# q and k of the first batch loaded as 2 KB runs and transposed head by head against the identity, with 14 unread matmuls ahead

## The chip, the cores and the metric

The kernel runs on one core of one Trainium2 chip. The metric is the device time of one execution in microseconds (us). Before the change three runs took 983.35, 987.0 and 985.17 us, median 985.17 us.

## The reference

An attention with two branches feeds a two-layer perceptron. Batch B = 8, heads H = 8, sequence S = 576, head dimension D = 64, inner width 2048, all in float32. The "down" branch averages q, k and v over groups of 4 tokens and attends over the 144 averages; the local branch lets each token attend to the 7 tokens around it.

```python
q_d = q.reshape(B, H, Sd, factor, D).mean(axis=3)     # k_d, v_d alike; factor 4, Sd 144
out_up = np.repeat(sm_attn(q_d, k_d, v_d), factor, axis=2)
mask = np.abs(pos[:, None] - pos[None, :]) < factor
scores = np.where(mask, scale * np.matmul(q, k.transpose(0, 1, 3, 2)), -1000000000.0)
x = (out_up + softmax(scores) @ v).transpose(0, 2, 1, 3).reshape(B * S, H * D)
h = x @ w_in
g = np.maximum(h, 0.0) + alpha * np.minimum(h, 0.0)
return g @ w_out
```

The weights arrive as 64-bit numbers and are decoded to float32 on the core.

## The kernel before, in words

The 4608 token rows are cut into 18 chunks of 256. For each chunk the perceptron runs in 8 steps, so there are 144 steps in all. `hidden` (L775) of a step does 24 matmuls of 128x256 (L784) for w_in, in three terms: high part by high part, high by low, low by high. `slopes` (L788) evacuates the result on ACT (ScalarE): two rows `t` (L799) and two rows `sh` (L801, in the early steps). `larger` (L807) adds them, in the early steps on POOL (GpSimd, L76), `split` (L813) makes the high part `gh` on ACT (L816) and the low part `gl` on POOL (L73), and `product` (L833) does 12 matmuls of 128x512 (L845) for w_out. The inputs `xh` and `xl` of the perceptron are the high and low part of the attention's output.

**Decoding the weights** (`make`, L175). Each of 16 blocks (8 of w_in, 8 of w_out, 1 MB raw each) goes through ACT (`magnitude`, L197), four DVE (VectorE) rows into the tile `temp` (L201, L202, L206, L207), ACT (`upper`, L212 or L216) and DVE (`lower`, L220 or twice L224). Raw data comes through three buffers, so the DMA of a block waits on the queue of SP (SyncE) until the block three earlier has been read. The first five blocks of each matrix are decoded in the first stage.

**The first batch** (`first_batch`, L385) is done differently from the other seven, on PE (TensorE), head pair by head pair, and it fills chunks 0 and 1. `load_pair` (L411) loads q, k and v of two heads. Each of q and k comes in two DMAs, one per head, into a tile laid out as (72 partitions, q or k, 8 tokens, 2 heads, 64): a partition holds 8 tokens, and each run that a descriptor carries is one token of one head, 64 floats or 256 bytes. The v of both heads comes in one DMA with runs of 8 tokens, 2048 bytes. `load_windows` (L421) loads v again in windows of 70 keys, in runs of 256 bytes. `pair` (L441) then does, for each head pair:

- q and k transposed on PE (L447): for each of 8 tokens one transpose of 72x128 (both heads at once), four to a PSUM tile, the tiles `f0T` (q) and `f1T` (k); ACT copies them to `qb` (L451) and `kT` (L455);
- window scores on PE: the mask by an identity matrix `unit` (L463), then q by k (L467);
- the sums over 4 tokens, folded in place on DVE in two rows each: q and k in L475 and L477, v in L493 and L495; then `fsum` (L482), down scores `fsd` (L491) and their softmax (`down_probs`, L339);
- the window softmax on DVE (L503 to L510) and ACT (L506), its transposes `fpt` (L515), the products `fdv` (L523) and `fpv` (L531), and on DVE the sum of both branches `fxs` (L534); ACT makes `xh` of it (L540) and DVE `xl` (L541).

**The order of the work.** `ORDER` (L40) lists the loads of the first batch on SP's queue: `i0` is a block of w_in, `o0` one of w_out, `a` a `load_pair`, `b` a `load_windows`. SP issues DMAs in that order and each waits for its buffer. All compute of the first stage and every event with a due time under `LISTED` = 14 (L50) is handed to a scheduler that works out the order of each engine's instructions; from step 14 on the order is that of the event list, written down by hand. Each engine works through its own order strictly, and a row that waits holds up all that stand behind it.

The down branch of the second batch (`down`, L237) starts inside the first stage: loads `ld` on SP (L247), folds on POOL (L76).

Of the kernel before, what the change touches and what calls it, by code (L numbers as in the profile page):

```python
# [9 lines left out]
F32 = mybir.dt.float32  # L10
# [3 lines left out]
ALU = mybir.AluOpType  # L14
# [9 lines left out]
HEAD = S * D  # L24
SEG = 18
NF = DF // 128
T = 256
# [21 lines left out]
FAR = {3: 2, 4: 2, 5: 2, 6: 2}  # L49
LISTED = 14  # L50
JOINS = (0.04, 0.06)


@with_exitstack
def tile_attention_moe(ctx: ExitStack, tc: tile.TileContext, q, k, v, w_in, w_out, alpha, out):
    nc = tc.nc

    const = ctx.enter_context(tc.tile_pool(name="const", bufs=1))
    one = ctx.enter_context(tc.tile_pool(name="one", bufs=1))
# [3 lines left out]
    ps_h = ctx.enter_context(tc.tile_pool(name="ps_h", bufs=2, space=PS))  # L63
    ps_a = ctx.enter_context(tc.tile_pool(name="ps_a", bufs=1, space=PS))

    def bank(kind, name):
        return ps_a.tile([128, 512], F32, tag=f"p{kind}", name=name, bufs=2 if kind == "d" else 1)
# [18 lines left out]
    ident = const.tile([128, 128], F32, name="ident")  # L86
# [298 lines left out]
    def first_batch(st):  # L385
# [13 lines left out]
        unit = st.tile([128, 128], F32R, name="unit")  # L399
# [9 lines left out]
        qk, vt, vw = {}, {}, {}  # L409

        def load_pair(hp):  # L411
            qk[hp] = one.tile([72, 2, 8, 2, 64], F32, tag=f"spare{(4, 5, 0, 1)[hp]}", name=f"fqk{hp}")
            for i, src in enumerate((q, k)):
                for e in range(2):
                    nc.sync.dma_start(qk[hp][:, i, :, e, :],
                                      bass.AP(src.tensor, (2 * hp + e) * HEAD, [[512, 72], [64, 8], [1, 64]]))
            vt[hp] = st.tile([72, 2, 8, 64], F32, tag="vt", name=f"fv{hp}", bufs=3)
            nc.sync.dma_start(vt[hp].rearrange("p h t d -> p h (t d)"),
                              bass.AP(v.tensor, 2 * hp * HEAD, [[512, 72], [HEAD, 2], [1, 512]]))
# [14 lines left out]
        def pair_bank(kind, name):  # L434
            if kind == "o":
                return ps_o.tile([128, 512], F32, tag="po", name=name)
            if kind == "h":
                return ps_h.tile([128, 512], F32, tag="ph", name=name)
            return bank(kind, name)

        def pair(hp):  # L441
            halves = [slice(64 * e, 64 * e + 64) for e in range(2)]
            for x in range(2):
                for t0, nt in ((0, 4), (4, 4)):
                    ps = ps_h.tile([128, 512], F32, tag="ph", name=f"f{x}T{hp}{t0}")[:, 0:72 * nt]
                    for i in range(nt):
                        nc.tensor.transpose(ps[:, 72 * i:72 * i + 72],  # L447
                                            qk[hp][:, x, t0 + i].rearrange("p h d -> p (h d)"), ident[:72, :72])
                    if x == 0:
                        for e, r in enumerate(halves):  # L450
                            nc.scalar.copy(  # L451
                                qb[r, :, e, :].rearrange("p w (a t) -> p w a t", t=8)[:, :, :, t0:t0 + nt],
                                ps[r].rearrange("p (t w a) -> p w a t", t=nt, w=NWIN))
                    else:
                        nc.scalar.copy(  # L455
                            kT[:, 3:S + 3].rearrange("p (a t) -> p a t", t=8)[:, :, t0:t0 + nt],
                            ps.rearrange("p (t a) -> p a t", t=nt))
            for part in ("sd", "ds")[EM[hp] == "b"]:
                if part == "s":
                    banks = []  # L460
                    for w0, nw in ((0, 7), (7, 2)):
                        ps = bank("q" if w0 == 0 else "l", f"fs{hp}{w0}")
                        nc.tensor.matmul(ps[:, 0:KEYS * nw], unit,  # L463
                                         wmask[:, w0:w0 + nw].rearrange("p w j -> p (w j)"), start=True, stop=False)
                        for i in range(nw):
                            w = w0 + i
                            nc.tensor.matmul(ps[:, KEYS * i:KEYS * i + KEYS], qb[:, w].rearrange("p e i -> p (e i)"),  # L467
                                             kT[:, WIN * w:WIN * w + KEYS], start=False, stop=(i == nw - 1))
                        banks.append((w0, w0 + nw, ps[:, 0:KEYS * nw].rearrange("p (w j) -> p w j", j=KEYS)))
                else:  # L470
                    sums = []
                    for i, x in enumerate("qk"):
                        lv = qk[hp][:, i].rearrange("p (g f) h d -> p g (f h d)", g=2)
                        s4 = lv[:, :, 0:256]
                        nc.vector.tensor_tensor(s4, lv[:, :, 0:256], lv[:, :, 256:512], op=ALU.add)  # L475
                        s2 = st.tile([72, 2, 128], F32, tag=f"fs2{x}", name=f"fs2{x}{hp}")
                        nc.vector.tensor_tensor(s2, s4[:, :, 0:128], s4[:, :, 128:256], op=ALU.add)  # L477
                        sums.append(s2)
                    ps = ps_h.tile([128, 512], F32, tag="ph", name=f"fsum{hp}")
                    for x in range(2):  # L480
                        for g in range(2):
                            nc.tensor.transpose(ps[:, (2 * x + g) * 72:(2 * x + g) * 72 + 72], sums[x][:, g],  # L482
                                                ident[:72, :72])
                    for e, r in enumerate(halves):
                        nc.scalar.mul(qd[r, :, 48 * e:48 * e + 48].rearrange("p b (i g) -> p b i g", g=2),
                                      ps[r, 0:144].rearrange("p (g b i) -> p b i g", g=2, b=3), DSCALE)
                    kd = st.tile([128, 144], F32, tag="fkh", name=f"fkd{hp}")
                    nc.scalar.copy(kd, ps[:, 144:288])
                    sd = bank("d", f"fsd{hp}")[:96, 0:432].rearrange("p (b c) -> p b c", b=3)
                    for bl in range(3):  # L490
                        nc.tensor.matmul(sd[:, bl, :], qd[:, bl, :], kd, start=True, stop=True)  # L491
            lv = vt[hp].rearrange("p h (g f) d -> p (h g) (f d)", g=2)
# [8 lines left out]
            p = st.tile([128, NWIN, KEYS], F32, tag="p", name=f"fp{hp}", bufs=2)  # L501
            for a_, b_, s in banks:
                nc.vector.tensor_reduce(out=mx[:, a_:b_], in_=s, axis=AX.X, op=ALU.max)  # L503
                nc.vector.tensor_tensor(p[:, a_:b_], s, mx[:, a_:b_].unsqueeze(2).to_broadcast([128, b_ - a_, KEYS]),
                                        op=ALU.subtract)
# [6 lines left out]
            for w0, nw in ((0, 4), (4, 4), (8, 1)):  # L512
                ps = pair_bank(FPT[hp][w0 // 4], f"fpt{hp}{w0}")
# [6 lines left out]
            for g in range(2):  # L520
                for e, r in enumerate(halves):
                    pr = th[g].rearrange("p (b e a) -> p b e a", b=3, e=2)[:, :, e]
                    nc.tensor.matmul(po[r, 0:144].rearrange("p (b a) -> p b a", b=3), vd[:, e, g], pr,  # L523
                                     start=(g == 0), stop=(g == 1))
            odf = st.tile([128, SD], F32, tag="odf", name=f"fod{hp}")
            nc.scalar.copy(odf, po[:, 0:144])
            for w0, nw in ((0, 4), (4, 4), (8, 1)):
                ps = pair_bank(FPV[hp][w0 // 4], f"fpv{hp}{w0}")
# [13 lines left out]
            yield  # L542

        return load_pair, load_windows, pair


# [340 lines left out]
    with tc.tile_pool(name="start", bufs=1) as start:  # L887
        load_pair, load_windows, pair = first_batch(start)
        todo = [(w, fp) for fp in range(NP) for w in range(2)]
        for step in ORDER.split():  # L890
            kind, i = step[0], int(step[1])
# [39 lines left out]
    t = T0_DEC  # L931
# [7 lines left out]
    for p in range(4 * (B - 1)):  # L939
        b, hp = 1 + p // 4, p % 4  # L940
# [12 lines left out]
    def flip_at(u, i, t, flip):  # L953
        when_flipped[u, i] = t
        at(t, flip, i)

    put = None
    for u in range(3, 3 * B + 1):
# [7 lines left out]
        elif put and u == 4:  # L966
            for i in range(2):
                flip_at(u - 1, i, begin[u] + 0.02 + 0.01 * i, flip)
                put(i, begin[u] + JOINS[i])
        elif put:  # L970
# [66 lines left out]
```

## Time and profile before

| | |
|---|---|
| median of three runs | 985.17 us |
| the profiled execution: its own time | 982.8 us |
| its span, first to last instruction | 981.0 us |
| PE matmul busy | 942.9 us (96%) |
| PE weight loads busy | 842.0 us (86%) |
| DVE busy | 819.5 us (84%) |
| ACT busy | 555.3 us (57%) |
| POOL busy | 527.6 us (54%) |
| mean granted TensorE clock | 0.976 |
| DMA packets | 63197, of these 23556 under 512 bytes |

All stretches and rows below are times from the span's start. A row of the timeline gives its start and its length in us, the engine, the line, the operation with its tiles, the count, and in brackets how long the engine was idle before it and what ended that. A row of the table by stretches gives, after the stretch and its length, the busy time of PE, PEld (weight loads), DVE, ACT and POOL with the number of instructions, the granted clock, the mean busy share of the 16 DMA engines and GB/s. One float32 matmul is two records on PE; a transpose, and a matmul on float32r operands (all of L463, L784 and L845), is one. PE's records overlap, so the pace of a group is its length over its count, and not the mean length of one.

### The profile page before, as it was taken

The numbers are of one execution on the slowest core, as the hardware profiler recorded it, in microseconds if no ns is written. First come the engines' busy times: TensorE is split into PE (matmuls) and PEld (weight loads), VectorE is DVE, ScalarE is ACT, GpSimd is POOL, SyncE is SP. The second block draws the span as 40 slices with busy tenths as digits, with TensorE's granted clock in tenths as the row PEclk, the third lists the DMA queues.
The fourth block names the chain that finished last, engine by engine and source line by source line (L and its number), as shares of the span: only waits on it lengthen the run. The fifth ranks groups of instructions, "written<-read, shape, count | busy, mean of one in ns | idle before, by whom it ended". The sixth has DMA issues, their size and how long they took to land.

```text
span 981.0 us, 17943 instructions
## 1 busy us (share of the span) xinstructions
PE 942.9 (96%) x6402; PEld 842.0 (86%) x6402; DVE 819.5 (84%) x1318; ACT 555.3 (57%) x1483; POOL 527.6 (54%) x642
## 2 busy tenths in 40 slices
PE   5878999999999999999999999999999999999998
PEld 4757887987888888989988899898899989999997
DVE  7999978888879999998889899899898889997111
ACT  4767776544645655556554655565556664544442
POOL 2055877787887546555537365555466633323221
PEclk9956999999999999999999999999999999999999
DMA  8946723132333322422322423332333321310000
GB/s 200 232 146 208 254 90 107 61 114 85 111 101 116 114 76 88 139 80 83 119 78 86 127 86 93 108 98 68 105 112 103 110 63 46 97 34 22 1 22 22
DMA packets 63197, 98.28 MB, mean 100 GB/s; under 512 B 23556, under 2 KB 28932, under 8 KB 63108
## 3 DMA queue, kind: packets, MB, share of 16 engines
q1 hardware_dynamic: 62916, 96.88, 32.8%
q8 instruction: 50, 0.82, 0.3%
q10 hardware_dynamic: 192, 0.26, 0.1%
q14 instruction: 39, 0.32, 0.1%
HBM read 87.67 MB, written 9.44 MB: 99 GB/s over the span
## 4 chain that ended last, share of the span: by engine, by line
PE 59%; DVE 11%; POOL 4%; ACT 3%; issue 2%; DMA 1%; SPq 0%; DVEq 0%; POOLq 0%
PE o L845 28%; PE h L784 27%; DVE lb L673 3%; DVE pv L670 2%; DVE qk L614 1%; PE s L278 1%; PE pv L312 1%; DVE t L811 1%; DVE ls L618 1%; PE xp L682 1%; POOL t L76 1%; PE pT L302 1%; DVE xf L698 1%; ACT t L799 1%; POOL gl L73 1%
## 5 line engine op out<-in xcount | busy, mean ns | idle before, releaser
L73 POOL TENSOR_TENSOR gl<-t,gh 128x512 fp32r<-128x512 f32 x144 | 186.3, 1294 | 323.4 <-ACT gh L816 303.3
L799 ACT ACTIVATE t<-h,slope 128x256 f32<-128x256 f32 x288 | 136.3, 473 | 128.8 <-PE h L784 105.7
L845 PE MATMUL o<-woh,gh 128*128 128x512 f32 x576 | 192.8, 405 | 2.5 <-ACT gh L816 1.1
L784 PE MATMUL h<-xh,wih 128*128 128x256 f32 x1152 | 188.0, 285 | 2.6 <-ACT sh L801 1.9
L845 PE MATMUL o<-wol,gh 128*128 128x512 f32 x576 | 185.7, 393 | 0.0
L845 PE MATMUL o<-woh,gl 128*128 128x512 f32 x576 | 185.4, 393 | 0.0
L784 PE MATMUL h<-xh,wil 128*128 128x256 f32 x1152 | 180.7, 279 | 0.0
L784 PE MATMUL h<-xl,wih 128*128 128x256 f32 x1152 | 180.5, 279 | 0.0
L784 PEld LDWEIGHTS h<-xh,wih 128*128 128x128 f32 x1152 | 162.8, 190 | 13.0 <-ACT sh L801 2.6
L816 ACT CAST gh<-t 128x512 fp32r<-128x512 f32 x144 | 89.5, 622 | 140.3 <-DVE t L811 81.6
L76 POOL TENSOR_TENSOR ld<-ld 72x256 f32<-72x256 f32 x168 | 131.9, 787 | 67.4 <-DMA ld<-in_q 64.8
L784 PEld LDWEIGHTS h<-xh,wil 128*128 128x128 f32 x1152 | 155.3, 190 | 0.3
L784 PEld LDWEIGHTS h<-xl,wih 128*128 128x128 f32 x1152 | 154.6, 190 | 0.1
L811 DVE TENSOR_TENSOR t<-h,t 128x512 f32<-128x512 f32 x114 | 78.3, 687 | 88.2 <-ACT h L803 87.8
L618 DVE TENSOR_REDUCE ls<-qk 128x12 f32<-128x768 f32 (+1 forms) x126 | 136.2, 1083 | 3.1
L845 PEld LDWEIGHTS o<-woh,gl 128*128 128x128 f32 x576 | 108.0, 188 | 24.0
L845 PEld LDWEIGHTS o<-wol,gh 128*128 128x128 f32 x576 | 108.0, 188 | 23.1 <-DVE temp L207 0.2
L673 DVE TENSOR_TENSOR lb<-lb,pv 128x384 f32<-128x384 f32 x202 | 114.0, 564 | 5.9
L845 PEld LDWEIGHTS o<-woh,gh 128*128 128x128 f32 x576 | 99.1, 188 | 18.9 <-issue 2.6
L803 ACT ACTIVATE h<-h,sign 128x256 f32<-128x256 f32 x228 | 100.2, 439 | 0.0
L670 DVE TENSOR_TENSOR pv<-v,lb 128x1152 f32<-128x1152 f32 x84 | 93.6, 1115 | 2.7
L614 DVE TENSOR_TENSOR qk<-k,qp 128x768 f32<-128x768 f32 (+1 forms) x78 | 84.0, 1078 | 4.6 <-ACT qp L607 4.6
(151 smaller groups left out, 1185.7 us busy)
## 6 DMA issues: line engine op xcount, KB each, us to landing
k<-in_k SPq DMA_DIRECT2D x41, 384.0 KB
v<-in_v SPq DMA_DIRECT2D x41, 384.0 KB
out<-sg SPq DMA_DIRECT2D x140, 64.0 KB
raw<-in_moe_w_in SPq DMA_DIRECT2D x16, 512.0 KB
raw<-in_moe_w_out SPq DMA_DIRECT2D x16, 512.0 KB
ld<-in_q SPq DMA_DIRECT2D x56, 144.0 KB
ld<-in_k SPq DMA_DIRECT2D x56, 144.0 KB
ld<-in_v SPq DMA_DIRECT2D x56, 144.0 KB
```

What stands on the lines that cost most here:

```text
L73: nc.gpsimd.tensor_tensor(o, a, b, op=ALU.subtract)
L76: nc.gpsimd.tensor_tensor(o, a, b, op=ALU.add)
L614: nc.vector.tensor_tensor(st["pr"][:, :nd], window(tiles[u, "k"], half, d0, nd), st["qp", half].unsqueeze(1).to_broadcast([128, nd, 2, 192 ...
L618: nc.vector.tensor_reduce(out=st["s"][:, half, d0:d0 + nd, :].rearrange("p a b -> p (a b)"), in_=st["pr"][:, :nd].rearrange("p a h (t d) - ...
L670: nc.vector.tensor_tensor(st["pr"][:, :nd], window4(tiles[u, "v"], half, d0, nd), prob(half, d0, nd), op=ALU.mult)
L673: nc.vector.tensor_tensor(st["acc"], st["acc"], st["pr"][:, i], op=ALU.add)
L784: nc.tensor.matmul(ph[:, j], w[:, m, 128 * o:128 * o + 128], x[:, m, :], start=(i == 0), stop=(i == 11))
L799: nc.scalar.activation(t[:, j], hs[st][:, j], AF.Copy, scale=slope[:, f:f + 1])
L803: nc.scalar.activation(other[:, j], hs[st][:, j], AF.Copy, scale=sign[:, f:f + 1])
L811: nc.vector.tensor_tensor(gs[st], hs.pop(st), gs[st], op=ALU.max)
L816: nc.scalar.copy(gh, t)
L845: nc.tensor.matmul(outs[c][m], g[:, j, 128 * m:128 * m + 128], wo[w][n][:, o, :], start=(f == 0 and i == 0), stop=(f == NF - 1 and i == 2))
```

## The change

The two DMAs for q of a head pair become one, with runs of 2048 bytes, and so do those for k. The tile is laid out head by head: (72, q or k, 2 heads, 8 tokens, 64), as that of v already is. In place of one transpose for both heads stand two float32 matmuls, one per head, of 64 columns against the identity, each into its own half of PSUM's partitions. The DVE folds of q and k go over the same 512 and 256 elements for each partition in the new layout. Ahead of the very first q tile, 14 matmuls of 128x512 multiply `unit` by itself into the same PSUM tile, which is then written over.

```diff
+WARM = 14
...
         def load_pair(hp):
-            qk[hp] = one.tile([72, 2, 8, 2, 64], F32, tag=f"spare{(4, 5, 0, 1)[hp]}", name=f"fqk{hp}")
+            qk[hp] = one.tile([72, 2, 2, 8, 64], F32, tag=f"spare{(4, 5, 0, 1)[hp]}", name=f"fqk{hp}")
             for i, src in enumerate((q, k)):
-                for e in range(2):
-                    nc.sync.dma_start(qk[hp][:, i, :, e, :],
-                                      bass.AP(src.tensor, (2 * hp + e) * HEAD, [[512, 72], [64, 8], [1, 64]]))
+                nc.sync.dma_start(qk[hp][:, i].rearrange("p h t d -> p h (t d)"),
+                                  bass.AP(src.tensor, 2 * hp * HEAD, [[512, 72], [HEAD, 2], [1, 512]]))
...
-                    ps = ps_h.tile([128, 512], F32, tag="ph", name=f"f{x}T{hp}{t0}")[:, 0:72 * nt]
+                    ps = ps_h.tile([128, 512], F32, tag="ph", name=f"f{x}T{hp}{t0}")
+                    if (hp, x, t0) == (0, 0, 0):
+                        for _ in range(WARM):
+                            nc.tensor.matmul(ps.rearrange("p (a n) -> p a n", a=4), unit,
+                                             unit.unsqueeze(1).to_broadcast([128, 4, 128]), start=True, stop=True)
+                    ps = ps[:, 0:72 * nt]
                     for i in range(nt):
-                        nc.tensor.transpose(ps[:, 72 * i:72 * i + 72],
-                                            qk[hp][:, x, t0 + i].rearrange("p h d -> p (h d)"), ident[:72, :72])
+                        for e, r in enumerate(halves):
+                            nc.tensor.matmul(ps[r, 72 * i:72 * i + 72], qk[hp][:, x, e, t0 + i], ident[:72, :72], start=True, stop=True)
...
-                        lv = qk[hp][:, i].rearrange("p (g f) h d -> p g (f h d)", g=2)
-                        s4 = lv[:, :, 0:256]
-                        nc.vector.tensor_tensor(s4, lv[:, :, 0:256], lv[:, :, 256:512], op=ALU.add)
+                        lv = qk[hp][:, i].rearrange("p h (g f) d -> p (h g) (f d)", g=2)
+                        s4 = lv[:, :, 0:128]
+                        nc.vector.tensor_tensor(s4, lv[:, :, 0:128], lv[:, :, 128:256], op=ALU.add)
                         s2 = st.tile([72, 2, 128], F32, tag=f"fs2{x}", name=f"fs2{x}{hp}")
-                        nc.vector.tensor_tensor(s2, s4[:, :, 0:128], s4[:, :, 128:256], op=ALU.add)
+                        s4 = s4.rearrange("p (h g) c -> p h g c", h=2)
+                        nc.vector.tensor_tensor(s2.rearrange("p g (h d) -> p h g d", h=2), s4[:, :, :, 0:64], s4[:, :, :, 64:128], op=ALU.add)
```

The scheduler works out the first stage anew, so rows move on every engine up to where the hand-written order begins. In the changed file line numbers stand 1 higher up to `load_pair` and 6 higher after the folds; rows of the change below carry its own numbers. The three places that follow are those that the prediction speaks of.

SP, the first loads of q, k and v after the first block of w_in (`fqk` is the tile of q and k, `fv` that of v), before:

```order
L415 DMA fqk_154<-in_q 72x8x64 x2
L415 DMA fqk_154<-in_k 72x8x64 x2
L418 DMA fv_159<-in_v 72x2x512
L415 DMA fqk_161<-in_q 72x8x64 x2
L415 DMA fqk_161<-in_k 72x8x64 x2
L418 DMA fv_166<-in_v 72x2x512
```

and in the change:

```order
L415 DMA fqk_154<-in_q 72x2x512
L415 DMA fqk_154<-in_k 72x2x512
L418 DMA fv_157<-in_v 72x2x512
L415 DMA fqk_159<-in_q 72x2x512
L415 DMA fqk_159<-in_k 72x2x512
L418 DMA fv_162<-in_v 72x2x512
```

Four fewer DMAs stand ahead of the second pair's v; the order of the rest of the first loads is the same.

DVE, the rows up to `xl` of the last head pair in chunk 0 (L541 before, L547 in the change), on which the first steps of the perceptron wait (`wol` and `wil` are the low parts of w_out and w_in, `temp` is the tile of the decode), before:

```order
L220 TENSOR_TENSOR wil_855<-temp,wih_854 128x4x256
L534 TENSOR_TENSOR fxs_796<-fpv_787,fod_785 128x256
L206 SCALAR_TENSOR_TENSOR temp<-raw_3_882,temp 128x1024
L282 TENSOR_REDUCE dnb_0_1082<-s_0_1067 96x3
L534 TENSOR_TENSOR rest<-fpv_813,fod_785 128x64
L201 TENSOR_SCALAR temp<-temp 128x1024
L541 TENSOR_TENSOR xl_108<-fxs_796,xh_107 128x256
```

and in the change:

```order
L225 SCALAR_TENSOR_TENSOR wol_937<-temp,sign,woh_936 128x512
L203 TENSOR_SCALAR temp<-temp 128x1024
L225 SCALAR_TENSOR_TENSOR wol_937<-temp,sign,woh_936 128x512
L540 TENSOR_TENSOR fxs_866<-fpv_857,fod_855 128x256
L207 SCALAR_TENSOR_TENSOR temp<-raw_4_964,temp 128x1024
L202 TENSOR_SCALAR temp<-temp 128x1024
L283 TENSOR_REDUCE dnb_0_1152<-s_0_1137 96x3
L540 TENSOR_TENSOR rest<-fpv_883,fod_855 128x64
L547 TENSOR_TENSOR xl_108<-fxs_866,xh_107 128x256
```

Ahead of this `xl`, DVE has in the change one decode block's rows more than before (one each of the lines 201, 202, 206 and 207 and two of line 224, in the numbers of before); all else ahead of it is the same work.

ACT, the evacuation of step 0 of the perceptron (`t` and `sh`, out of the hidden tile `h`), before:

```order
L297 ACTIVATE dp_0_1090<-dp_0_1090,drs_0_1084 96x144 x3
L799 ACTIVATE t_1019<-h_994,slope 128x256
L197 ACTIVATE temp<-raw_4_906 128x1024
L801 ACTIVATE sh_1020<-h_994,gain 128x256
L799 ACTIVATE t_1019<-h_994,slope 128x256
L801 ACTIVATE sh_1020<-h_994,gain 128x256
```

and in the change:

```order
L298 ACTIVATE dp_0_1160<-dp_0_1160,drs_0_1154 96x144 x3
L805 ACTIVATE t_1089<-h_1064,slope 128x256
L807 ACTIVATE sh_1090<-h_1064,gain 128x256
L805 ACTIVATE t_1089<-h_1064,slope 128x256
L807 ACTIVATE sh_1090<-h_1064,gain 128x256
```

The decode row of the fifth w_out block (L197) no longer stands between the four evacuations; it comes earlier.

## The prediction

> **What bounds the kernel now.** The first view is the chain of waits, summed by engine: a list of engines with the share of the span that lies on each.
>
> ```profile
> PE 59%; DVE 11%; POOL 4%; ACT 3%; issue 2%; DMA 1%; SPq 0%; DVEq 0%; POOLq 0%
> ```
>
> PE carries most of it, but the change lies in the first stage, so that stage has to be read by itself. The second view is the table by stretches.
>
> ```profile
> 4.00:6.00 2.00, 0.00 (x0) 0.00 (x0) 1.75 (x5) 0.00 (x0) 1.82 (x6) 1.00 1.02 360
> 10.00:20.00 10.00, 8.94 (x46) 7.71 (x45) 8.16 (x14) 5.76 (x14) 0.00 (x0) 1.00 1.01 231
> 20.00:30.00 10.00, 7.95 (x42) 7.43 (x42) 9.53 (x19) 5.54 (x16) 0.00 (x0) 1.00 0.97 174
> 30.00:40.00 10.00, 10.00 (x107) 8.83 (x105) 7.87 (x18) 8.21 (x26) 0.00 (x0) 1.00 1.10 238
> 40.00:46.00 6.00, 4.58 (x49) 3.22 (x46) 6.00 (x15) 5.90 (x18) 0.00 (x0) 1.00 0.96 338
> 46.00:86.00 40.00, 31.61 (x208) 24.56 (x209) 39.64 (x63) 27.91 (x69) 14.70 (x13) 0.51 0.49 163
> 86.00:100.00 14.00, 11.08 (x77) 10.17 (x77) 13.97 (x17) 9.58 (x21) 13.95 (x12) 0.83 0.71 231
> 100.00:150.00 50.00, 48.63 (x340) 43.54 (x339) 42.86 (x63) 37.61 (x99) 39.87 (x47) 1.00 0.47 155
> ```
>
> Three things are to be seen. From 40 to 100 us DVE (third of the busy columns) has no gap worth the name: 6.00 of 6, 39.64 of 40, 13.97 of 14. Behind 100 us PE takes over, 48.63 of 50. And from 4 to 46 us the DMA engines are full (share 0.96 to 1.10) although they move only 174 to 238 GB/s in the three stretches from 10 to 40, against 360 from 4 to 6, where the 4 KB rows of the first weight block go: full of small packets, not of bytes. So up to 100 us the question is when DVE gets through, and there its waits are the third view.
>
> ```profile
> DVE fv L493 <- DMA fv<-in_v: 3.9, 2, 2.1
> DVE temp L201 <- ACT temp L197: 2.5, 3, 1.8
> ```
>
> The fourth, the timeline, places them.
>
> ```profile
> 2.89 1.86 SPq L415 DMA_DIRECT2D fqk<-in_q  x2
> 4.79 2.67 SPq L415 DMA_DIRECT2D fqk<-in_k  x2
> 7.51 0.62 SPq L418 DMA_DIRECT2D fv<-in_v  x1
> 8.77 0.69 DVE L201 TENSOR_SCALAR temp<-temp 128x1024 f32<-128x1024 f32 x1 [1.80 <-ACT temp L197]
> 9.23 1.19 PE L447 MATMUL f0T<-ident,fqk 72*128 72x72 f32 x8 [9.23 <-DMA fqk<-in_q]
> 17.20 0.69 DVE L493 TENSOR_TENSOR fv<-fv 72x512 f32<-72x512 f32 x1 [1.81 <-DMA fv<-in_v]
> 23.39 0.69 DVE L201 TENSOR_SCALAR temp<-temp 128x1024 f32<-128x1024 f32 x1 [0.43 <-ACT temp L197]
> 34.42 0.69 DVE L493 TENSOR_TENSOR fv<-fv 72x512 f32<-72x512 f32 x1 [2.10 <-DMA fv<-in_v]
> ```
>
> DVE starts its real work at 8.77, waiting for the first weight block, which stands ahead of q on the queue and doesn't change. Behind that it loses 1.81 and 2.10 to the v of the second and fourth pair and 0.43 to a raw block whose decode began late: **4.34 us** in all. All three stand behind the q and k loads on one queue.
>
> **The loads.** The pair's q and k take 1.86 + 2.67 us of SP's queue today; v, which has the new form already (one DMA, runs of 2 KB), takes 0.62. Three such issues instead of five take 1.9 where 5.2 stood, 3.3 us less for each pair. The bytes of one q or k load are 72 x 2 x 2048 = 295 KB; at the 360 GB/s of the 4-to-6 row that is 0.8 us of the DMA engines, where 1.3 to 1.7 would be needed at 174 to 231 GB/s. The v of the second pair then lands some 6 us sooner and that of the fourth more, since each pair ahead gives time back; both waits were 2 us. So I take all 4.34 us off DVE's path: **-4.3**. What is late next on DVE is nothing up to 46 us that the rows show, ACT and PE being further from full. The window loads of v (256-byte runs) stay on the queue; if they alone keep it full, none of the 4.3 comes back.
>
> **The folds.** They keep their element counts, with the middle dimension split.
>
> ```profile
> 10.22 0.69 DVE L475 TENSOR_TENSOR fqk<-fqk 72x512 f32<-72x512 f32 x1
> 12.30 0.68 DVE L493 TENSOR_TENSOR fv<-fv 72x512 f32<-72x512 f32 x1
> ```
>
> The fold of v has the very shape that q and k get, and costs the same: 0.
>
> **PE's own work.** A transposed tile is four records today, sixteen in the change (eight float32 matmuls). Nearest rows, the window products being also 64 columns of weights with 64 to 72 moving ones:
>
> ```profile
> 12.98 4.11 PE L467 MATMUL fs<-kT,qb 128*128 128x70 f32 x18
> 16.89 0.69 PE L447 MATMUL f0T<-ident,fqk 72*128 72x72 f32 x4
> 33.28 0.43 PE L447 MATMUL f1T<-ident,fqk 72*128 72x72 f32 x4
> 35.29 0.69 PE L531 MATMUL fpv<-fpT,vw 70*64 70x64 f32 x16
> 37.17 1.33 PE L467 MATMUL fs<-kT,qb 128*128 128x70 f32 x10
> 66.64 1.65 PE L531 MATMUL fpv<-fpT,vw 70*64 70x64 f32 x20
> 103.08 0.39 PE L845 MATMUL o<-woh,gh 128*128 128x512 f32 x1
> 103.31 0.39 PE L845 MATMUL o<-wol,gh 128*128 128x512 f32 x1
> ```
>
> PE has two paces. The score products take 4.11/18 = 228 ns a record up to about 30 us and 1.33/10 = 133 at 37; the transposes of a tile 0.69 at 17 and 0.43 at 33. The clock column says 1.00 at both, so before 32 us I go by the durations. A new tile is 16 records in 0.69 us at the fast pace (the row at 35) and 16 x 1.65/20 = 1.3 at the slow one (the row at 67, where the column says 0.51). There are 16 tiles. If the pace is fast from the start: a tile costs 0.69 where the slow transposes cost 0.69, and a row of 18 score products falls from 4.11 to 18 x 0.133 = 2.4, so PE has less to do than now up to 32 us; after that 16 - 8 tiles x 0.26 = 2 us more, beside a DVE that has none free. I take 0 here. The 14 unread matmuls start when `unit` is ready, about 2.5 us, and take 14 x 0.23 (the distance of the two rows at 103) = 3.2 us, at half pace 6.4; they end at 5.7 to 8.9, and q lands at 9.2 now and some 0.8 sooner in the change: 0, at worst 0.5 on an engine that DVE doesn't wait for there. Whether they hold the pace for tiles that come afterwards is a rival below.
>
> [...]
>
> **The order.** The change's order puts one more decode block on DVE ahead of the last pair's `xl`.
>
> ```profile
> 10.83 1.22 DVE L206 SCALAR_TENSOR_TENSOR temp<-raw,temp 128x1024 int32<-128x1024 int32 x1
> 30.71 0.74 DVE L224 SCALAR_TENSOR_TENSOR wol<-temp,sign,woh 128x512 fp32r<-128x512 f32 x1
> 84.55 0.41 DVE L541 TENSOR_TENSOR xl<-fxs,xh 128x256 fp32r<-128x256 f32 x1
> 92.69 0.73 PE L784 MATMUL h<-xh,wih 128*128 128x256 f32 x4 [1.87 <-ACT sh L801]
> 94.99 1.05 PE L784 MATMUL h<-xh,wil 128*128 128x256 f32 x4
> 99.36 0.51 PE L845 MATMUL o<-woh,gh 128*128 128x512 f32 x1 [1.05 <-ACT gh L816]
> 99.66 4.40 DVE L220 TENSOR_TENSOR wil<-temp,wih 128x1024 fp32r<-128x1024 f32 x1
> 100.46 0.74 PE L784 MATMUL h<-xh,wih 128*128 128x256 f32 x4
> 102.40 0.62 PE L784 MATMUL h<-xh,wil 128*128 128x256 f32 x4
> 126.79 0.51 PE L784 MATMUL h<-xh,wih 128*128 128x256 f32 x2 [0.70 <-ACT wih L212]
> 149.13 0.74 PE L845 MATMUL o<-woh,gh 128*128 128x512 f32 x2 [0.67 <-ACT woh L216]
> ```
>
> Six rows: 2 x 0.69 + 2 x 1.22 + 2 x 0.74 = 5.3 us. So that `xl` is done at 84.55 - 4.3 + 5.3: **+1.0** later. But the block done there isn't done later. Between the first hidden step and the one at 100.46 PE loses 1.87 (held by `sh`, behind the decode row that the order takes away), 1.05 (held by `gh`), some 0.3 in small gaps, and 3 x 0.43 = 1.3 because three groups of four go at 1.05 instead of 0.62: 4.5 in all. With the block and the ACT row gone from between, I expect most of it back and take 3.6, all but the small gaps and half of the slow pace: 1.0 - 3.6 = **-2.6** at the step now at 100.46. Behind it two waits of PE for decoded weights, 0.70 and 0.67, are left; DVE's rows up to them are the same work, so they shrink only by what DVE is ahead there, and I take **-0.4** of their 1.4. The sum is **-3.0**, carried to the end because PE is full behind 100. Bounds: nothing back, +1.0; all 4.5 and both waits, 1.0 - 4.5 - 1.4 = -4.9. The decode row at 99.66 takes 4.40 where another of its kind takes 1.22, beside a POOL that is full in that stretch; whether the new order meets POOL more or less is unknown, and 3 us either way is its bound.
>
> The profiled execution took 982.8 us, 2.4 under the median of 985.17. From its own 982.8 the sum gives 979.8; on the median it gives 985.17 - 3.0 = **982.2**, say 982.
>
> **The rivals.**
> - *All comes back and more* (faster): every loss of the last part and the 3.2 us that the row at 99.66 is over its kind: -4.9 - 3.2, less the part of that row which PE doesn't wait for, about -7: 978. For it, DVE is the bound until there; against it, behind 100 us DVE has 7 us of 50 free, so its long rows are half covered.
> - *The loads change nothing that ends last* (no change): the 2 KB runs free the queue, but the window loads and the weight blocks fill it again, or the gain is eaten by the extra block. Then between 0 and 5.3 - 3.6 - 0.4 = +1.3: 985 to 986.5. For it, the DMA share of about 1 up to 46 us; against it, the v that is late is exactly behind q and k.
> - *PE becomes the bound of the first pairs* (slower): the unread matmuls end before q lands, PE idles, the slow pace comes back and a tile costs 1.3. Then 16 x (1.3 - 0.69) = 9.8 us more on PE, which has only 30 - 26.9 = 3.1 free from 10 to 40; of the 6.7 beyond, the 8.4 free us from 46 to 86 take about a third, so +4: 989. It decides if a tile of q or k takes over about 1.0 us through the second pair. Against it, the change's matmuls are of the kind behind which the pace was fast at 35.
>
> **How the numbers follow.** Forecast 0.47, faster rival 0.20, no change 0.21, slower rival 0.12. The predicted time is 982. About 0.5%, 4.9 us, is what a measurement of this kernel can tell from no change; that puts the border at 980.3. The forecast's own spread (POOL, 3 us) lets some 0.11 of its 0.47 fall under it, and the first rival some 0.16 of its 0.20: faster 0.27; the third rival and little else lie above 990: slower 0.08; the same 0.65. For the range, the upper end takes in the no-change case and nearly half of the slower one, 988.5; the lower all of the forecast's spread and most of the first rival, 975.5.
>
> **What would show it.** In the profile of the changed kernel: the first tile of q on PE starts before 8.6; a tile's 16 records take 0.8 or less through pair two; DVE's waits between 9 and 40 us sum to under 0.8; the last `xl` of chunk 0 comes at about 85.5; the hidden step now at 100.46 starts near 97.9; behind 100 us PE's rows are the same but for the shift. The forecast is wrong if DVE still waits for v, if PE's gaps between 10 and 40 close, or if the step now at 100.46 comes at its old time although DVE got through sooner.

## The result: slower by 1.1%, and the profile after

| | before | change |
|---|---|---|
| median | 984.26 us (4 runs, 982.95 to 987.0) | 994.89 us (4 runs, 991.46 to 999.91) |
| ratio to before, 95% interval | | 1.0108, 1.0059 to 1.0158 |
| profiled execution, its span | 982.8, 981.0 us | 994.99, 993.2 us |
| PE matmul busy | 942.9 us | 956.8 us |
| mean granted clock | 0.976 | 0.956 |

The change costs 10.6 us where 3 us less were forecast; the time lies outside the range of 975.5 to 988.5. The first view is again the table by stretches, now of the change, with the same columns as in the prediction.

```profile
4.00:6.00 2.00, 2.00 (x6) 1.60 (x5) 1.76 (x5) 0.00 (x0) 1.82 (x6) 1.00 0.98 337
10.00:20.00 10.00, 9.07 (x102) 8.28 (x99) 7.42 (x11) 3.76 (x8) 0.00 (x0) 0.57 0.94 231
20.00:30.00 10.00, 7.78 (x69) 6.14 (x66) 6.52 (x14) 5.13 (x12) 0.00 (x0) 0.50 0.91 186
30.00:40.00 10.00, 9.53 (x90) 8.48 (x89) 7.78 (x16) 6.43 (x22) 0.00 (x0) 0.50 1.08 228
40.00:46.00 6.00, 6.00 (x31) 4.34 (x30) 5.59 (x11) 4.13 (x8) 0.00 (x0) 0.53 0.94 326
100.00:150.00 50.00, 40.45 (x272) 36.43 (x271) 31.64 (x52) 31.69 (x77) 34.67 (x40) 0.93 0.54 181
```

DVE is busy less than before from 20 to 30 us (6.52 of 10 instead of 9.53), the clock stands at half from 11.46 to 45.60 us, where ten of the sixteen tiles of q and k are transposed, and between 100 and 150 us, where PE was full, 9.6 of 50 us are now idle. The waits of DVE between 8 and 100 us, in the change (us in total, how often, the longest):

```profile
DVE fv L499 <- DMA fv<-in_v: 5.6, 4, 2.3
DVE temp L202 <- ACT temp L198: 4.3, 3, 2.7
DVE fmx L509 <- PE fs L472: 0.7, 1, 0.7
DVE wol L225 <- ACT woh L217: 0.7, 1, 0.7
DVE fvd L501 <- PE fdv L529: 0.4, 1, 0.4
```

The first row was to go, and of the second the part behind DVE's start (0.43); both grew (3.9 and 2.5 before). The five rows sum to 11.7 us, where they were 6.4. The timeline of the change shows the places; its line numbers stand 1 to 6 higher.

```profile
2.50 6.04 PE L448 MATMUL f0T<-unit 128*128 128x512 f32 x14 [2.50 <-ACT unit L401]
8.49 1.12 ACT L198 ACTIVATE temp<-raw 128x1024 f32<-128x1024 f32 x1 [6.05 <-DMA raw<-in_moe_w_in]
9.65 0.69 DVE L202 TENSOR_SCALAR temp<-temp 128x1024 f32<-128x1024 f32 x1 [2.66 <-ACT temp L198]
9.82 1.22 PE L453 MATMUL f0T<-ident,fqk 72*64 72x72 f32 x32 [1.28 <-DMA fqk<-in_q]
17.52 0.69 DVE L499 TENSOR_TENSOR fv<-fv 72x512 f32<-72x512 f32 x1 [1.07 <-DMA fv<-in_v]
19.09 1.23 PE L453 MATMUL f0T<-ident,fqk 72*64 72x72 f32 x16
34.18 0.69 DVE L499 TENSOR_TENSOR fv<-fv 72x512 f32<-72x512 f32 x1 [0.82 <-DMA fv<-in_v]
94.55 0.41 DVE L547 TENSOR_TENSOR xl<-fxs,xh 128x256 fp32r<-128x256 f32 x1
110.81 1.52 POOL L77 TENSOR_TENSOR ld<-ld 72x256 f32<-72x256 f32 x2 [3.36 <-DMA ld<-in_q]
112.29 1.26 POOL L77 TENSOR_TENSOR t<-sh,t 128x512 f32<-128x512 f32 x1
114.25 0.79 PE L851 MATMUL o<-woh,gh 128*128 128x512 f32 x1 [8.20 <-ACT gh L822]
```

From top to bottom: the unread matmuls ran at half pace (6.04/14 = 431 ns each); DVE starts on the first weight block 0.9 us later than before (in the runs below its start lies between 8.50 and 9.71 us with either kind of load, so the loads are not shown to be the cause); the first two tiles of q came at 9.82, not sooner than 9.23, and took 1.22 us together, at the fast pace; v of the second and fourth pair is folded at 17.52 and 34.18, where it was at 17.20 and 34.42; a tile of the second pair takes 1.23 us; the last pair's `xl` comes ten microseconds late; and then PE stands 8.20 us because POOL's sum `t` of the first step stands behind folds of the second batch that wait for their load.

### The profile page after: what moved, and what is told of

Read it like the earlier page. It is cut to its first block, busy times and chain, and to the rows that moved or that the text cites. A ratio compares the mean times of both kernels' runs of the same rounds, so it can differ in the third digit from the quotient of the medians.

```text
span 993.2 us, 18347 instructions
## 1 busy us (share of the span) xinstructions
PE 956.8 (96%) x6608; PEld 854.1 (86%) x6608; DVE 813.5 (82%) x1318; ACT 556.7 (56%) x1483; POOL 533.6 (54%) x642
## 4 chain that ended last, share of the span: by engine, by line
PE 55%; DVE 13%; POOL 4%; ACT 3%; issue 2%; DMA 1%; SPq 0%; DVEq 0%; POOLq 0%; ACTq 0%
PE o L851 26%; PE h L790 25%; DVE lb L679 3%; DVE pv L676 2%; DVE qk L620 2%; DVE ls L624 2%; DVE t L817 1%; PE s L279 1%; PE pv L313 1%; PE xp L688 1%; POOL t L77 1%; DVE xf L704 1%; ACT t L805 1%; PE pT L303 1%; POOL gl L74 1%
## 5 line engine op out<-in xcount | busy, mean ns | idle before, releaser
L77 POOL TENSOR_TENSOR ld<-ld 72x256 f32<-72x256 f32 x168 | 134.1, 801 | 73.9 <-DMA ld<-in_q 70.2
L790 PEld LDWEIGHTS h<-xh,wih 128*128 128x128 f32 x1152 | 162.5, 190 | 11.7 <-ACT sh L807 1.6
```

Source lines behind the costliest of these rows:

```text
L77: nc.gpsimd.tensor_tensor(o, a, b, op=ALU.add)
L790: nc.tensor.matmul(ph[:, j], w[:, m, 128 * o:128 * o + 128], x[:, m, :], start=(i == 0), stop=(i == 11))
```

## The experiments

The scheduler makes a new order for every change of the first stage, so a plain variant mixes the change with its order. Most kernels below therefore hold the order of each engine in the first stage to a recorded one ("order of before" or "order of the change"): an edge between each instruction and the next, issue order only, no wait. Two records that replace one stay together. The diffs below show each edit without these edges.

```diff
+PIN = {"Pool": "...", "SP": "...", "DVE": "...", "Activation": "...", "PE": "..."}
...
+    for name, text in PIN.items():
...
+        for a, z in zip(chain, chain[1:]):
+            tc.add_manual_dep(z, a.name, behind, reason="pinned")
```

All were timed in five rounds beside the kernel before, whose medians were 983.77 (runs 1 to 4), 983.42 (5 to 8), 983.15 (9 to 11) and 982.1 us (12).

**1. The whole change, order of before.** Edit: PIN of before on the change.

> The whole change (2 KB loads, identity matmuls, 14 unread matmuls), but every engine's instructions of the first stage held in the order of the kernel before. Theory ORDER (the 10.6 us come from the order that the scheduler makes for the change): the time is that of before or 1 to 4 us under it, the first product step starts at 97 to 100 us. Theory PACE (sixteen records a tile on a PE at half pace delay the first head pairs whatever the order): 991 to 996 us, the first product step at 105 to 110 us. Theory LOADS (2 KB loads crowd out the first weight block and v is no sooner): DVE starts at about 9.6 us and waits over 5 us for v, 986 to 990 us.

993.03 us, ratio 1.0089 (1.0061 to 1.0117). Its table by stretches:

```profile
30.00:40.00 10.00, 10.00 (x80) 8.09 (x77) 5.36 (x11) 6.33 (x16) 0.00 (x0) 0.50 1.05 202
40.00:46.00 6.00, 6.00 (x62) 5.30 (x60) 3.38 (x8) 3.19 (x11) 0.00 (x0) 0.50 1.03 315
46.00:60.00 14.00, 14.00 (x136) 11.92 (x137) 9.13 (x16) 8.37 (x21) 5.66 (x6) 0.50 0.17 45
```

PE has no gap from 30 to 60 us and DVE is busy 17.9 of 30: PE became the bound of the first batch. Two of DVE's new waits:

```profile
DVE rest L551 <- PE fpv L548: 1.9, 1, 1.9
DVE fqk L491 <- PE f0T L462: 1.8, 1, 1.8
```

The order cannot be the whole cause; ORDER falls as the only theory, PACE has its number and its first product (109.83). LOADS falls too: DVE starts at 8.50 and waits 3.1 us for v.

**2. The kernel before, order of the change.** Edit: PIN of the change on before.

> The old loads and the old transposes, nothing ahead of them, but every engine's instructions of the first stage held in the order that the scheduler makes for the change. ORDER: 992 to 997 us, with POOL's sum of the first step late behind a fold that waits for its load, as in the change. PACE: 984 to 987 us. LOADS: 984 to 988 us.

992.0 us, 1.0082 (1.0057 to 1.0107): old loads, old transposes, and nearly the same loss. So the order is a sufficient cause too. DVE's waits between 8 and 100 us:

```profile
DVE fv L510 <- DMA fv<-in_v: 7.4, 4, 3.0
DVE temp L210 <- ACT temp L206: 5.2, 4, 2.7
```

The order asks for v four times before it is there, and puts decode rows ahead of the attention. PE's pace is slow here too (a tile of four records takes 0.74 us at 37.85, where it took 0.47 at 35.91 before), but DVE waits only 0.8 us for PE, so that is not the cause. POOL's sum of the first step, which ORDER had named, holds PE up for 3.8 us and not for 8.2. The two losses, 9.3 and 8.2 us, do not add up: together they are 10.6. Where the stretches lie, by the timeline of each (us from the start), with the sum of all waits of DVE between 8 and 100 us:

| kernel | first `xl` of the first pair | `xl` of the last pair, chunk 0 | first product matmul | DVE's waits |
|---|---|---|---|---|
| before | 39.84 | 84.55 | 99.36 | 6.4 |
| change | 54.23 | 94.55 | 114.25 | 11.7 |
| 1: change, order of before | 44.24 | 95.06 | 109.83 | 16.6 |
| 2: before, order of the change | 55.47 | 96.40 | 110.98 | 13.4 |
| 4: 24 unread matmuls | 42.61 | 87.81 | 102.63 | 9.9 |
| 7: sum ahead | 57.48 | 96.63 | 111.03 | 15.0 |

In the order of before DVE waits for PE's tiles; in the order of the change it decodes first and the attention comes later. Either way the last `xl` is at about 95. The table adds up to within 2 us: less DVE's waits, that `xl` stands at 77.9 to 78.5 us in the order of before and at 81.6 to 83.0 in the order of the change, which has the decode rows of one block (5.3 us) more ahead of it.

**3 and 8. Without the unread matmuls.** Edit, in the order of before (3) and in that of the change (8):

```diff
-WARM = 14
+WARM = 0
```

> As the first, but with none of the 14 unread matmuls. If these are of no use because the clock falls back before the tiles come, the time is that of the first within 2 us. If their warm stretch from 8 to 11.5 us shortens the first pair, this one is 2 to 4 us slower. If they do harm (a clock that fell at 11.5 us rises later than one that never rose), it is 2 to 4 us faster.

> The change in its own order on every engine, without the 14 unread matmuls. If they are of no use there: 993 to 997 us, as the change. If their short warm stretch helps, 2 us or more over it; if it harms, 2 us or more under it.

989.59 us, 1.0064 (1.0032 to 1.0096), against 993.03 of run 1; and 992.71 us, 1.0087 (1.0062 to 1.0111), against 994.89 of the change. Both lie lower without them, but the intervals overlap: the 14 matmuls show no gain, and whether they harm is not settled.

**4. 24 unread matmuls instead of 14, order of before.**

```diff
-WARM = 14
+WARM = 24
```

> As the first, but with 24 unread matmuls instead of 14, so that they reach up to the first tile of q (about 9.8 us). PACE: the clock stays at 1.00 behind 11.5 us, a tile of 16 records takes about 0.7 instead of 1.23 us and the time falls 4 to 8 us under that of the first. ORDER: the pace of PE is covered by DVE, so the clock may rise but the time is that of the first within 2 us.

989.5 us, 1.0068 (1.0034 to 1.0101), but the eight executions fall into two groups: four from 985.19 to 987.43 with a mean clock of 0.968 to 0.972, four from 991.57 to 996.24 with 0.956 to 0.967. The profile is of the first group (986.63):

```profile
10.00:20.00 10.00, 8.78 (x142) 7.38 (x142) 8.38 (x14) 5.96 (x14) 0.00 (x0) 1.00 0.92 216
20.00:30.00 10.00, 4.91 (x37) 4.39 (x36) 7.81 (x17) 4.82 (x14) 0.00 (x0) 0.67 0.90 178
30.00:40.00 10.00, 10.00 (x104) 8.18 (x105) 6.81 (x13) 6.96 (x17) 0.00 (x0) 0.65 1.02 210
40.00:46.00 6.00, 6.00 (x92) 5.30 (x90) 5.40 (x15) 4.20 (x14) 0.00 (x0) 1.00 1.10 276
```

With the clock up for most of the stage the work gets through 7 us sooner than in run 1 (87.81 against 95.06 in the table), and the execution is still 2.9 us over the median of before. So in this execution the pace is most of the price of the sixteen records in this order, as PACE had it; only half of the executions come out so.

**5. Identity matmuls alone.** Old loads, order of before.

```diff
-                        nc.tensor.transpose(ps[:, 72 * i:72 * i + 72],
-                                            qk[hp][:, x, t0 + i].rearrange("p h d -> p (h d)"), ident[:72, :72])
+                        for e, r in enumerate(halves):
+                            nc.tensor.matmul(ps[r, 72 * i:72 * i + 72], qk[hp][:, x, t0 + i, e], ident[:72, :72], start=True, stop=True)
```

> Only the transposes are replaced by two identity matmuls a token; loads as before, nothing unread, order of before. Theory RECORDS (sixteen records a tile instead of four make PE the bound of the first pairs): 988 to 992 us, DVE waits for PE between 10 and 60 us as in the third run, and the 2 KB loads are worth under 2 us either way. Rival LOADS HELP (the 2 KB loads give DVE's wait for v back and the identity matmuls cost that much more): 992 to 996 us, 2 KB loads worth 2 to 4 us. Rival LOADS HURT: 984 to 987 us.

995.37 us, 1.0098 (1.0064 to 1.0132): two executions at 987.62 and 989.16, four from 994.96 to 996.77. By its median this edit alone makes the whole loss; that number is the one of LOADS HELP (992 to 996), not of RECORDS. Run 3, which differs only in the 2 KB loads, is 5.8 us lower by its median, but with overlapping intervals and the same two groups (five from 987.73 to 990.16, two at 994.0 and 996.01). What the 2 KB loads are worth beside slow tiles is not settled; no loss by them shows.

The two groups can be seen in the traces: run 5 was profiled in an execution of its lower group (987.62) and run 3 in one of its upper group (994.0). Both go through nearly the same rows at the slow pace up to 38 us. Then, in run 5,

```profile
38.07 0.72 PE L465 MATMUL f1T<-ident,fqk 72*64 72x72 f32 x16
```

and in run 3

```profile
38.63 1.23 PE L462 MATMUL f1T<-ident,fqk 72*64 72x72 f32 x16
```

where a tile still takes 1.18 at 43.56. The last `xl` comes at 88.57 in run 5 and at 95.27 in run 3; the executions differ by 6.4 us. In these two, then, the groups differ by how long PE's pace stays slow. The loads differ as well, so one trace of each group doesn't prove it for the rest, and why the pace rises when it does stays open.

**6. Unread matmuls alone.** 24 of them on the kernel before, nothing else.

> The kernel before in its own order, with 24 unread matmuls ahead of the first tile of q and nothing else. RECORDS: DVE is the bound of the first stage there, so a clock that rises earlier changes nothing, 982 to 986 us. Rival (a slow PE holds back the kernel before too): 978 to 981 us.

982.64 us, 0.9994 (0.9975 to 1.0013): no difference. But the unread matmuls did not hold the pace: the first two tiles of q take 0.67 us (1.19 before), but a tile at 16.83 takes 0.69 as before, and the mean granted clock is 0.73 from 10 to 20 us and 0.50 from 20 to 30. They also hold the first tile of q up until 10.53, where it started at 9.23. So a faster PE from there to about 15 us is worth nothing here; what a fast one up to 30 us would be worth isn't shown.

**7. The sum ahead of the folds.** The change in its own order; in POOL's row of PIN, `t` and `gl` of step 0 are moved ahead of the folds of the second batch's third pair.

> The change in its own order, but on POOL the first step's sum and its low part go ahead of the three folds of the second batch's third head pair, which stood before them and between them. Theory ORDER (in the change's own order PE's wait of 8.2 us for that sum is a loss of its own): the wait shrinks to 1 to 3 us and the time falls by 4 to 6 us to 989 to 991. Rival (the wait only covers a later one, since PE then runs out of decoded weights): 993 to 996 us, with a new wait of PE between 110 and 130 us.

992.4 us, 1.0080 (1.0052 to 1.0107). PE's wait there went from 8.2 us to

```profile
PE o L862 <- ACT gh L833: 1.4, 1, 1.4
```

but the time fell by 2.5 us at the medians, with overlapping intervals, instead of 4 to 6. The profiled execution took 995.03 with the wait at 1.4, that of the change 994.99 with 8.2, and in run 8, in the same order, the wait is 3.9. The wait is at most a small part of the loss.

**9. The 2 KB loads without the identity matmuls.** One transpose takes two tokens of one head, and ACT puts the four quarters in place. Nothing unread, order of before.

```diff
+                        e, j = divmod(i, 2)
+                        nc.tensor.transpose(ps[:, 72 * i:72 * i + 72],
+                                            qk[hp][:, x, e, t0 + 2 * j:t0 + 2 * j + 2].rearrange("p t d -> p (t d)"), ident[:72, :72])
...
+                    for e, r in enumerate(halves):
+                        for a, p in enumerate(halves):
...
+                            else:
+                                nc.scalar.copy(
+                                    kT[r, 3:S + 3].rearrange("p (a t) -> p a t", t=8)[:, :, t0 + a:t0 + nt:2],
+                                    ps[p, 144 * e:144 * e + 144].rearrange("p (j a) -> p a j", j=2))
```

> The 2 KB loads without the identity matmuls: a transpose takes two tokens of one head (128 columns that lie together), so a tile is four transposes as before, and ACT copies it in four pieces instead of two or one; nothing unread, order of before. RECORDS (the loads themselves move little, the sixteen records a tile cost the time): 983 to 987 us, of which ACT's pieces may be 1 to 3. The prediction's step on the loads: 979 to 981 us, with DVE's waits for v gone. LOADS HURT (they push back the first weight block and the later loads): 988 to 992 us.

991.9 us, 1.0078 (1.0055 to 1.0102). The number is that of LOADS HURT, the trace says otherwise. DVE's waits between 8 and 46 us, in part, and the stretch from 20 to 30:

```profile
DVE fqk L493 <- PE f0T L462: 2.5, 2, 1.4
DVE temp L210 <- ACT temp L206: 1.7, 1, 1.7
DVE fmx L522 <- PE fs L485: 1.2, 4, 0.6
DVE fsm L526 <- ACT fp L525: 1.0, 1, 1.0
...
DVE fv L512 <- DMA fv<-in_v: 0.7, 1, 0.7
```

```profile
20.00:30.00 10.00, 5.51 (x28) 4.62 (x26) 6.56 (x15) 9.30 (x30) 0.00 (x0) 1.00 0.90 194
```

DVE starts at 8.68, so the first weight block isn't pushed back. The wait for v is down to 0.7 us, and ACT is full (9.30 of 10) with its pieces (1.21 us for a tile of q and 1.46 for one of k, where 0.81 and 0.47 stood before): the tiles wait for ACT, and DVE for the tiles. Four short copies in place of two or one cost more in this trace than the loads could give. So this run does not isolate the loads.

**10. Every transpose made twice.** The kernel before, order of before.

```diff
+                        for again in range(2):
-                        nc.tensor.transpose(ps[:, 72 * i:72 * i + 72],
-                                            qk[hp][:, x, t0 + i].rearrange("p h d -> p (h d)"), ident[:72, :72])
+                            nc.tensor.transpose(ps[:, 72 * i:72 * i + 72],
+                                                qk[hp][:, x, t0 + i].rearrange("p h d -> p (h d)"), ident[:72, :72])
```

> The kernel before in its own order, every transpose of q and k made twice into the same place: eight records a tile instead of four, about 1.4 us a tile at half pace, near the 1.23 of the identity matmuls; loads as before. RECORDS: as with the identity matmuls, 988 to 996 us, DVE waits for the tiles of PE between 10 and 60 us. Rival (it is what the identity matmuls are, not how long they take, for example what the clock makes of them): 983 to 987 us.

986.6 us, 1.0033 (1.0013 to 1.0053): slower by 3.4 us at the medians. That is the number of the rival (983 to 987), not of RECORDS. A tile takes as long as one of identity matmuls at half pace:

```profile
18.52 1.17 PE L465 MATMUL f0T<-ident,fqk 72*128 72x72 f32 x8
```

Later the pace rises here too (0.67 us for the eight records of a tile at 34.59). Eleven of twelve executions lie from 983.92 to 989.22, the two lower ones of run 5 at the upper end of that; one is at 993.48. So PE's time per tile at the slow pace is a cost of its own, some 3 to 5 us, with either kind of record, and the four upper executions of run 5 lose another 7 us that this kernel nearly always escapes. By the two traces under run 5 a pace that stays slow longer would account for them; the one trace of run 10 can't show it.

**11. Run 9 in the scheduler's order.**

> As the first of these three, but in the order that the scheduler makes for it. If an order made for these loads is as good as the one of before: within 2 us of the first. If new orders of the first stage lose as the one of the change does, 989 to 994 us. A version that beats both kernels would be at 981 us or under.

994.67 us, 1.0116 (1.0096 to 1.0136): another new order for the first stage, about as slow as the change and just above the 989 to 994 of new orders that lose. No version here beats before.

**12. v ahead of q and k.** The kernel before, order of before, on SP the v of the last three pairs moved ahead of their q and k.

> The kernel before in its own order, but v of the second, third and fourth head pair loaded ahead of that pair's q and k. It gives DVE's two waits for v (3.9 us) back without any change of the loads themselves. The later steps of the prediction's sum (DVE is the bound of the first stage, so what it no longer waits comes off the end): 979 to 981 us and the last low part of the first chunk about 4 us sooner. Theory CHAIN (the first stage is a chain that goes round PE, ACT and DVE, and DVE's waits for v are cover for tiles that aren't ready either; q and k now come 1 to 2 us later): 982 to 986 us, with new waits of DVE for PE in their place.

983.26 us, 1.0022 (0.9998 to 1.0046): no gain. DVE's waits between 8 and 100 us:

```profile
DVE temp L210 <- ACT temp L206: 3.8, 4, 1.7
DVE fqk L492 <- PE f0T L464: 0.9, 2, 0.6
DVE fsm L524 <- ACT fp L523: 0.8, 1, 0.8
DVE fmx L520 <- PE fs L484: 0.4, 1, 0.4
DVE fqk L492 <- PE f1T L464: 0.2, 1, 0.2
```

The 3.9 us for v are gone and 6.1 us of waits stand where 6.4 stood: for the decode, PE and ACT. The last `xl` of chunk 0 comes at 84.47, as before. The edit is not free, though: q and k of the later pairs are issued 0.4 to 1.8 us later, so part of the new waits may be its own.

## Why the prediction was wrong

**The loads, -4.3: the step that failed first.** DVE's waits up to the last `xl` were to shrink by 4.34 us; they grew by 5.3, from 6.4 to 11.7. I took a q or k load at the 360 GB/s of the stretch from 4 to 6 us. That is the pace of the weight block, and not of these loads. The DMA view between 9 and 15 us, before:

```profile
DMA packets 3084, 1.24 MB, mean 207 GB/s; under 512 B 2820, under 2 KB 2820, under 8 KB 3084
```

and in the change:

```profile
DMA packets 800, 1.27 MB, mean 211 GB/s; under 512 B 199, under 2 KB 199, under 8 KB 800
```

A quarter of the packets, and the bytes move no faster. SP's queue was freed (v of the second pair is issued at 5.51 instead of 12.00), but it only filled up sooner, and v landed when it had landed before (in runs 1, 3 and 9, with the same loads, v of the second pair is folded at 15.62 to 16.77, so 0.4 to 1.6 us sooner and not some 6). That the waits for v grew is the new order's doing: run 2 has it with the old loads, at 7.4 us. "Full of small packets, not of bytes" was a reading of two columns that stood beside each other, not a test.

**DVE as the bound up to 100 us: the step under it.** DVE's rows and waits do add up to the last `xl`, but a wait that goes doesn't come off that sum. In run 12 the 3.9 us for v are gone and nothing is gained. My own table had the row: from 30 to 40 us PE was at 10.00 of 10 and DVE at 7.87. Up to 46 us the stage is a chain that goes round PE, ACT and DVE, and its waits hide each other. I had called ACT and PE "further from full" there, against that row.

**PE's own work, taken at 0: wrong by most of the loss.** The price was right (1.23 us a tile, 1.3 forecast at the slow pace), the cover was not. Run 5 sets this edit at 12 us in the order of before; run 10, with the same time per tile, at 3.4. It is the third rival, with its deciding point (a tile over about 1.0 us through the second pair). Its +4 was too small: it counted the slow pace on the 16 tiles alone, and PE's other rows were slow too (16 of the window products take 1.12 us at 40.22 in run 1, 0.69 at 35.29 before). That the pace would be fast from the start, on which the 0 stood, was my own estimate, and no run of this change shows it: its tiles between 11.46 and 45.60 us, identity matmuls all of them, take 2.19 us for two and 1.17 to 1.23 for one, and in run 4, with 24 unread matmuls, a tile takes 0.72 up to 20.73 and 1.23 again at 35.89.

**The unread matmuls, 0: right.** They end at 8.54, inside the bounds, and q came at 9.82. The pace that they had raised (the first pair's two tiles of q took 1.22 us together, 2.19 in runs 3 and 8 without them) lasted for these two tiles; the clock fell at 11.46, and the tiles behind it were slow (1.23 us at 19.09). Runs 3 and 8 see no gain from them.

**The order, +1.0 - 3.6 - 0.4: wrong in size and sign.** The last `xl` was forecast at about 85.5 and came at 94.55. The 5.3 us of decode rows were counted rightly: 84.55 + 5.3 + 5.3 of added waits is 95.2. What was to give them back did not: the hidden step forecast near 97.9 came at 116.13. `t` and `gh` met a new wait, 8.20 us, which I had not looked for on POOL though I had its order. Run 2 puts the order at 8.2 us by itself. That its 5.3 us of decode rows are repaid later was half right: the block does not come later (`wil` of the fifth block at 98.29 instead of 99.66), but PE's steps came later all the same.

**The folds, 0: right** (0.68 us and 0.41 us in both traces; one row of the change takes 0.92).

Not settled: why PE's pace rises at 38 us in one execution and has not risen at 43.56 in another that does nearly the same, which seems to decide between the two groups of runs 3 and 5 (of run 4 only the lower group has a trace), and what the 2 KB loads are worth by themselves.

## What to carry to other kernels

A queue whose engines show a busy share of about 1 is not shown to be bound by its packets (here 3084 packets moved at 207 GB/s and 800 at 211): compare a stretch with large packets to and from the same tiles before pricing a load at another load's pace. Work added to an engine is hidden only if that engine has gaps in the stretch where the work falls (PE had none from 30 to 40 us, 10.00 of 10), and in a chain that goes round three engines a wait that goes can come back at the next one, as it did in run 12. Where a scheduler orders a stage, compare variants with the order held fixed, both ways: here the order alone and the new work alone each made nearly the whole loss.

## What the runs showed of the hardware that was not expected

The clock. In these traces the column says 1.00 up to the first change on record, whatever the pace is: the 14 unread matmuls stand in a stretch of 1.00 and took 431 ns each, where the same form takes 230 later (the rows at 103 in the prediction). So a high mean clock can hide a slow start: run 3's column is 1.00 from 10 to 60 us, with tiles at 1.2 us and the one at 43.56 still at 1.18, and the four upper executions of run 5 show 0.986 to 0.999, the two lower ones 0.978 and 0.979. Stretches of the change, cut at the unread matmuls' start and end, at the first tile of q and at the changes on record, 11.46 and 45.60, with two inside the slow stretch in which PE was full:

```profile
2.50:8.54 6.04, 6.04 (x14) 4.46 (x14) 2.67 (x10) 0.05 (x1) 3.66 (x16) 1.00 0.90 242
8.54:9.82 1.28, 0.00 (x1) 0.03 (x1) 0.17 (x1) 1.28 (x2) 0.00 (x0) 1.00 0.79 206
9.82:11.46 1.64, 1.64 (x35) 1.38 (x35) 1.22 (x2) 1.23 (x4) 0.00 (x0) 1.00 0.79 210
11.46:45.60 34.14, 30.52 (x245) 25.65 (x244) 25.91 (x46) 18.01 (x44) 0.00 (x0) 0.50 0.98 234
14.30:18.20 3.90, 3.90 (x18) 3.82 (x18) 2.83 (x6) 1.04 (x1) 0.00 (x0) 0.50 1.05 196
40.00:45.60 5.60, 5.60 (x27) 3.94 (x26) 5.23 (x10) 3.74 (x7) 0.00 (x0) 0.50 0.95 328
45.60:50.00 4.40, 4.40 (x79) 4.19 (x78) 3.95 (x8) 4.19 (x13) 0.00 (x0) 1.00 0.59 135
```

The clock fell at 11.46, 2.92 us after the last unread matmul and while PE was at work (1.64 of 1.64 us). It stayed at 0.50 for 34.1 us, in which PE was busy for 30.52, all the time from 14.30 to 18.20, and was back at 1.00 at 45.60, where PE had been full since 40.00. Before the change PE was busy for 4.58 of the 6 us from 40 to 46 with the column at 1.00, and the column is 0.50 from 46.45 to 50.00. What the fall and the rise hang on is not shown by these traces. So here the matmuls ahead of the work bought a pace that served two tiles (1.22 us) and was lost at 11.46.
